# Turning the keys of a gated attention token-major: from TensorE transposes to VectorE block transposes with sixteen placing transfers

## The chip, the core and the metric

The kernel runs on one core of a Trainium2 chip. The metric is the device time of one launch in microseconds (us); smaller is better. The engines are named as a profile names them: PE (TensorE matmul) and PEld (its weight loads), DVE (VectorE), ACT (ScalarE), POOL (GpSimd), SP (SyncE, which here only issues DMA transfers). Each engine runs its own instruction list strictly in order and waits where an operand is not ready.

## The reference, cut to what matters

```python
def attn(q, k, v, a_re, a_im):                # all (4, 8, 768, 48)
    mag = np.sqrt(a_re * a_re + a_im * a_im)
    scale = np.minimum(mag, 0.999) / (mag + 1e-06)
    a_re_n, a_im_n = a_re * scale, a_im * scale
    for t in range(S):
        ar, ai = a_re_n[:, :, t, :, None], a_im_n[:, :, t, :, None]
        new_re = ar * S_re - ai * S_im
        new_im = ar * S_im + ai * S_re
        kv = np.einsum('bhd,bhe->bhde', k[:, :, t], v[:, :, t])
        S_re, S_im = new_re + kv, new_im
        y[:, :, t] = np.einsum('bhd,bhde->bhe', q[:, :, t], S_re)
    return y

x = attn_out.transpose(0, 2, 1, 3).reshape(3072, 384)
out = ((x @ w_a) * (x @ w_b)) @ w_out         # w_a, w_b: 384 x 1536, w_out: 1536 x 384
```

A recurrence over 768 tokens with a complex gate per key channel (8 heads of 48 channels, 4 sequences), then a gated feed-forward layer.

## The kernel before

**Units.** The recurrence is cut into chunks of 128 tokens. A *unit* u is one chunk of two sequences (256 tokens); there are 12 units, 6 per pair of sequences (`c = u % 6` is the chunk). Three stages follow one another for each unit:

- `prep(u)`, mostly DVE: it normalises the gates of unit u+1 (`scale`, whose first step is a square on ACT, L178, and whose first DVE step is L179, its last L193), builds running products of the gates of unit u (L211 to L294) and their inverse (L297 to L320), and multiplies keys and queries in the tile `qk` with them (L324, then twice L309). At its end it loads the gates of unit u+2 into a tile `a_t` (L158). There are two `a_t` buffers, and `prep(u)` uses the one of its own unit as scratch.
- `stack(u)`: ten transfers on SP that copy `qk` into `stk`, head by head, real part above imaginary part (96 rows a head).
- `attn(u)`, for each of the two sequences i and each group of four heads: `scores` (PE L379, mask on DVE L382 into `am`), `transposes` (PE L390 turns the stacked keys token-major, ACT L394 copies them out of PSUM into `kt`), `outputs` (PE L422 from `am`, values, state and queries into `xp`; ACT L424 rounds it into `xh`, DVE L430 leaves the rest in `xl`), and `state` (PE L445 from `kt` and the values, DVE L452 adds to the state tiles `u_111`, `u_112`). In the last chunk of a sequence `transposes` and `state` are left out.

**Passes.** The feed-forward layer of unit w is pass w: 12 blocks f. A block is 18 matmuls (L489, weights of `w_a` and `w_b` in two parts each), a gate product (ACT L497, DVE L498, ACT L499, DVE L500 give `hh` and `hl`), and six matmuls (L507) that run two blocks behind. A pass needs all of `xh` and `xl` of its unit. During pass w the generators of `attn(w+1)`, of the end of `prep(w+2)` and of the start of `prep(w+3)` are drained a piece at a time between blocks. PSUM has three buffers for the L489 results (`ab`) and two (`pm`) that scores, transposes and states share.

**What sets the order.** The program is written in this interleaved order, but a scheduler with a cost model then fixes each engine's list before the launch; `tc.high_priority` raises the gate product and the attention's copies above the rest. In the finished program nothing moves any more: who is late makes everything behind it on its engine late.

**Layouts that the change touches.** Values come as 128 columns for each pair of heads, with zero columns in the middle (32 + 16 + 16 + 32 used); state tiles have the same columns.

Of the kernel before, what the change touches and what calls it, by code (L numbers as in the profile page):

```python
# [8 lines left out]
F32 = mybir.dt.float32  # L9
# [8 lines left out]
B, H, S, D = 4, 8, 768, 48  # L18
DM, DF = 384, 1536
# [4 lines left out]
NJ = 3  # L24
# [43 lines left out]
def tile_kernel(ctx: ExitStack, tc: tile.TileContext, a_d, qk_d, v_d, w_d, qn_d, kn_d, vn_d, an_d, out_d):  # L68
# [98 lines left out]
    def scale(u, a_t, tmp):  # L167

        sc = zpool.tile([128, W], F32, name="sc")
        for n, hs in enumerate(halves if u == 0 else (slice(0, W),)):
            n = n and NU
            t = tmp[:, 0:2, hs]
            m, x, s0 = t[:, 0], t[:, 1], sc[:, hs]
            act.activation(out=t, in_=a_t[:, :, hs], func=AF.Square, accum_out=sums[:, u + n:u + n + 1])  # L178
# [12 lines left out]
            vec.scalar_tensor_tensor(out=s0, in0=m, scalar=0.5, in1=s0, op0=ALU.add, op1=ALU.mult)
            yield 900
            vec.scalar_tensor_tensor(out=s0, in0=s0, scalar=0.999, in1=x, op0=ALU.mult, op1=ALU.min)  # L193
            yield 900
        sc_tiles[u] = sc

    def rescaled(c):
        return c % 2 == 1 and c + 1 < NCH

    def prep(u):  # L200
# [137 lines left out]
    def stack(u):  # L338
        n = RUN if rescaled(u % NCH) else 2 * TOK
        for h in range(H):  # L340
            r0 = h * D
            while r0 < (h + 1) * D:
                j, p = divmod(r0, 128)
                m = min((h + 1) * D - r0, 128 - p)
                d0 = 2 * (r0 - h * D)
                sync.dma_start(out=stk[d0:d0 + 2 * m, h, 0:n], in_=qk[p:p + m, j, :, 0:n])
# [12 lines left out]
    quads = [[] for _ in range(4)]
    for g in range(H // 2):  # L360
        for q, pieces in ((3 * g, [(2 * g, 0)]), (3 * g + 1, [(2 * g + 1, 96)]),
                          (3 * g + 2, [(2 * g, 32), (2 * g + 1, 64)])):
            quads[q % 4].append((q // 4, [(h, g * 128 + off) for h, off in pieces]))

    def attn(u, xh, xl):

        c = u % NCH
        last = c + 1 == NCH
        ams, kts, xps = {}, {}, {}

        def cols(i):
            return slice(i * C, (i + 1) * C), slice(TOK + i * C, TOK + (i + 1) * C)
# [13 lines left out]
        def transposes(i, hg):  # L386
            qs, ks = cols(i)
            tp = ps_m.tile([128, 512], F32, name="pm")
            for h4 in range(4):
                pe.transpose(out=tp[:, h4 * KS:(h4 + 1) * KS], in_=stk[0:KS, hg * 4 + h4, ks],  # L390
                             identity=ident[0:KS, 0:KS])
            kt = kvp.tile([128, 4, KS], F32, name="kt", bufs=2)
            with tc.high_priority(offset=ATTN_FIRST):
                act.copy(out=kt.rearrange("p h k -> p (h k)"), in_=tp[:, 0:4 * KS])  # L394
# [42 lines left out]
        def state(i, hg):  # L437
            ut, v_t = us[i], v_tiles[u, i]
            own = u >= OWN_FROM
            n = D if own else 2 * D  # L440
            kp = ps_m.tile([128, 512], F32, name="pm")
            for h4 in range(4):
                h = hg * 4 + h4
                o = (h // 2) * 128 + (h % 2) * (80 if own else 32)
                pe.matmul(out=kp[0:KS, h4 * n:(h4 + 1) * n], lhsT=kts[i, hg][:, h4, :],  # L445
                          rhs=v_t[:, o:o + n], start=True, stop=True)
            uv = view(ut[0:KS], hg * 256, [[128, 2], [80, 2], [1, 48]])
            kv = view(kp[0:KS], 0, [[2 * n, 2], [D if own else 3 * D, 2], [1, D]])
            sv = view(stk[0:KS], hg * 4 * RUN + 2 * TOK + i, [[2 * RUN, 2], [RUN, 2], [0, 48]])
            with tc.high_priority(offset=ATTN_FIRST):  # L450
                if c > 0:
                    vec.tensor_tensor(out=uv, in0=kv, in1=uv, op=ALU.add)  # L452
                else:
                    act.copy(out=uv, in_=kv)
                if rescaled(c):
                    vec.tensor_tensor(out=uv, in0=uv, in1=sv, op=ALU.mult)
# [8 lines left out]
                     (residual, 1, 0), (state, 0, 0), (state, 0, 1), (transposes, 1, 0), (transposes, 1, 1),  # L465
                     (state, 1, 0), (state, 1, 1)]
        for fn, i, g in order:
            if not (last and fn in (transposes, state)):
                fn(i, g)
                yield  # L470

    def pieces(u):
        return 8 if u % NCH + 1 == NCH else 16

    def new_x():
        return (moe.tile([128, NJ, TOK], F32, name="xh"), moe.tile([128, NJ, TOK], F32, name="xl"))
# [3 lines left out]
        m, b = divmod(blk, NJ)  # L480
        return w_t[f, m][:, part, b * 128:(b + 1) * 128]

    def gemm1(f, xh, xl, ps_ab=ps_ab, moe=moe):
        ab = ps_ab.tile([128, 512], F32, name="ab")
        for m in range(2):
            n = 0
            for i in range(NJ):
                for part, xt in ((0, xh), (0, xl), (1, xh)):
                    pe.matmul(out=ab[:, m * TOK:(m + 1) * TOK],  # L489
                              lhsT=r(w_ab(f, part, m * NJ + i)),  # L490
                              rhs=r(xt[:, i, :]), start=n == 0, stop=n == 8)
                    n += 1
        h_t = moe.tile([128, TOK], F32, name="h_t")
        hh = moe.tile([128, TOK], F32, name="hh", bufs=HB)
        hl = moe.tile([128, TOK], F32, name="hl", bufs=HB)
        with tc.high_priority(offset=MOE_FIRST):
            act.copy(out=h_t, in_=ab[:, 0:TOK])  # L497
            vec.tensor_tensor(out=h_t, in0=ab[:, TOK:2 * TOK], in1=h_t, op=ALU.mult)  # L498
            act.copy(out=r(hh), in_=h_t)  # L499
            vec.tensor_tensor(out=r(hl), in0=h_t, in1=hh, op=ALU.subtract)  # L500
        return hh, hl
# [148 lines left out]
    for w in range(NU):  # L650
        last = w + 1 == NU
        x_nxt = None if last else new_x()
        at = None if last else attn(w + 1, *x_nxt)
        if not last:
            load_v(w + 1)
        os_ = [ps_o.tile([128, 512], F32, name=f"o{t}") for t in range(2)]
        slots = [0, 2 * (STACK_AT[min(w, 4)] + 1 - max(ATTN_AT[min(w, 4)], 0 if w else P1_AT + 1))]
        left = [pieces(w + 1)]

        def slot():  # L660
            if at is None or f < ATTN_AT[min(w, 4)] or (w == 0 and f <= P1_AT) or not slots[1]:
                return
            n = -(-left[0] // slots[1])
            slots[1] -= 1
            for _ in range(n):
                next(at, None)
                left[0] -= 1

        for f in range(NF):
            if w == 0:  # L670
                next(ws, None)
                drain(p1, P1_F)
                if f == P1_AT:
# [4 lines left out]
            pend.append((w, f, *gemm1(f, *x_cur), os_))  # L678
# [89 lines left out]
```

## Time and profile before

| | |
|---|---|
| median of 3 runs | 690.6 us (690.31 to 691.74) |
| the profiled execution | 690.18 us, of which 688.5 us are the span that the profile covers |
| granted TensorE clock | 0.972 of full speed over the span |
| instructions | 14290 |
| DMA packets | 30232, 63.94 MB |

The profile is of one execution. Its page gives busy time by engine, the span in 40 slices, the chain of work that ended last and the costliest groups of instructions. Further views are the windows (busy time by engine in a stretch of the span), the timeline of an engine, the waits and the list of DMA issues. A busy PE is not PE at its peak, since matmuls are pipelined: two matmuls of 280 ns each may start 120 ns apart.

### The profile page before, as it was taken

To read this page: it belongs to the slowest core of one execution; us is meant where nothing else is said; L and a number is where in the kernel's file an instruction comes from. 1 tells how busy PE (TensorE), PEld (TensorE's weight loads), DVE (VectorE), ACT (ScalarE), POOL (GpSimd) and SP (SyncE) were. 2 spreads that over 40 slices of the span, in tenths; PEclk is the share of its full clock that TensorE was granted. 3 is DMA by queue.
4 is the path that set the end of the run, shared out by engine and by line. 5 is a ranking of instruction groups with operands and counts; after the bars stand their busy time and mean duration, and the time that the engine had idled before them with its cause. 6 is when DMAs were issued, how large, how long until landed. Compare 5 with 4: busy or idle time off the path is not lost.

```text
span 688.5 us, 14290 instructions
## 1 busy us (share of the span) xinstructions
PE 644.5 (94%) x5842; PEld 608.3 (88%) x5842; DVE 550.1 (80%) x1259; ACT 310.1 (45%) x622; POOL 5.6 (1%) x11
## 2 busy tenths in 40 slices
PE   3547999999999999999999999999999999999996
PEld 1214889899999999999999999999999999999996
DVE  6999899998989989999898898999989963233221
ACT  7357664735445346354363553635542332221221
POOL 3000000000000000000000000000000000000000
PEclk9676999999999999999999999999999999999999
DMA  8963301513314225043160440611500500400000
GB/s 321 402 268 95 121 1 44 143 54 87 115 39 139 63 78 145 16 136 104 29 194 2 122 117 3 178 60 62 155 24 18 153 24 18 108 24 2 24 1 28
DMA packets 30232, 63.94 MB, mean 93 GB/s; under 512 B 3664, under 2 KB 7248, under 8 KB 30160
## 3 DMA queue, kind: packets, MB, share of 16 engines
q1 hardware_dynamic: 26704, 58.23, 27.3%
q10 hardware_dynamic: 3456, 4.72, 1.9%
q8 instruction: 48, 0.79, 0.5%
q14 instruction: 24, 0.20, 0.1%
HBM read 39.32 MB, written 4.72 MB: 64 GB/s over the span
## 4 chain that ended last, share of the span: by engine, by line
PE 66%; DVE 25%; ACT 4%; DMA 2%; issue 2%; SPq 0%; DVEq 0%; ACTq 0%
PE ab L489 33%; PE o L507 16%; PE xp L422 5%; PE pm L379 4%; PE pm L445 3%; DVE a_t L289 3%; DVE qk L309 2%; PE pm L390 2%; DVE h_t L498 2%; DVE hl L500 2%; PE pm L147 1%; DVE z L294 1%; DVE pr L227 1%; DVE am L382 1%; DVE pb L262 1%
## 5 line engine op out<-in xcount | busy, mean ns | idle before, releaser
L489 PE MATMUL ab<-xh,w 128*128 128x256 f32 x1728 | 341.6, 286 | 0.0
L489 PEld LDWEIGHTS ab<-xh,w 128*128 128x128 f32 x1728 | 277.2, 189 | 1.7 <-issue 0.8
L489 PE MATMUL ab<-xl,w 128*128 128x256 f32 x864 | 245.5, 284 | 0.0
L489 PEld LDWEIGHTS ab<-xl,w 128*128 128x128 f32 x864 | 163.0, 189 | 0.6 <-issue 0.2
L507 PE MATMUL o<-w,hh 128*128 128x384 f32 x576 | 152.7, 343 | 0.0
L497 ACT COPY h_t<-ab 128x256 f32<-128x256 f32 x144 | 53.4, 371 | 163.4 <-PE ab L489 163.4
L498 DVE TENSOR_TENSOR h_t<-ab,h_t 128x256 f32<-128x256 f32 x144 | 60.4, 420 | 64.6 <-ACT h_t L497 64.3
L507 PEld LDWEIGHTS o<-w,hh 128*128 128x128 f32 x576 | 96.6, 188 | 1.1 <-issue 1.0
L507 PE MATMUL o<-w,hl 128*128 128x384 f32 x288 | 97.2, 338 | 0.0
L499 ACT CAST hh<-h_t 128x256 fp32r<-128x256 f32 x144 | 58.0, 403 | 78.0 <-DVE h_t L498 76.9
L500 DVE TENSOR_TENSOR hl<-h_t,hh 128x256 fp32r<-128x256 f32 x144 | 60.4, 419 | 16.6 <-ACT hh L499 16.4
L379 PE MATMUL pm<-stk 128*128 128x128 f32 x384 | 54.8, 280 | 2.1 <-DMA stk<-qk 2.0
L147 PE MATMUL ab<-o_sb,ident 128*128 128x384 f32 x42 | 28.1, 764 | 29.7 <-DVE o_sb L138 29.7
L379 PEld LDWEIGHTS pm<-stk 128*128 128x128 f32 x384 | 50.2, 194 | 5.7 <-issue 3.6
L507 PEld LDWEIGHTS o<-w,hl 128*128 128x128 f32 x288 | 54.1, 188 | 0.0
L227 DVE TENSOR_TENSOR pr<-z 128x384 f32<-128x384 f32 (+1 forms) x91 | 47.2, 525 | 1.8
L289 DVE TENSOR_TENSOR a_t<-z,b_t 128x768 f32<-128x768 f32 x48 | 44.7, 947 | 0.1
L147 PEld LDWEIGHTS ab<-o_sb,ident 128*128 128x128 f32 x42 | 9.5, 268 | 39.3 <-DVE o_sb L138 30.3
L309 DVE TENSOR_TENSOR qk<-qk,z 128x1536 f32<-128x1536 f32 (+1 forms) x26 | 42.3, 1626 | 0.2
L422 PE MATMUL xp<-am,v_t 128*32 128x128 f32 x768 | 37.7, 281 | 4.3 <-DVE am L382 4.1
L382 DVE TENSOR_TENSOR am<-pm,mask 128x512 f32<-128x512 f32 x48 | 32.7, 685 | 5.2 <-PE pm L379 4.4
L424 ACT CAST xh<-xp 128x384 fp32r<-128x384 f32 x24 | 11.4, 475 | 49.3 <-PE xp L422 49.1
(107 smaller groups left out, 768.7 us busy)
## 6 DMA issues: line engine op xcount, KB each, us to landing
w<-in_dram SPq DMA_DIRECT2D x36, 384.0 KB, 8.0
qk<-in_dram SPq DMA_DIRECT2D x12, 768.0 KB, 4.9
stk<-qk SPq DMA_DIRECT2D x48, 192.0 KB, 3.3
a_t<-in_dram SPq DMA_DIRECT2D x11, 768.0 KB, 4.3
v_t<-in_dram SPq DMA_DIRECT2D x24, 256.0 KB, 2.7
stk<-qk SPq DMA_DIRECT2D x24, 192.8 KB, 3.3
out_dram<-o_sb ACTq DMA_DIRECT2D x24, 192.0 KB, 1.9
stk<-qk SPq DMA_DIRECT2D x16, 128.0 KB, 3.1
```

What stands on the lines that cost most here:

```text
L147: pe.matmul(out=lp[:, 0:n], lhsT=ident, rhs=t, start=True, stop=False)
L227: vec.tensor_tensor(out=pr[:, :, :, o:o + n], in0=view(zz, W + at_(i) + 2 * o, [[W, 2], [-W, 2], [2, n]]), in1=tok(slice(1, 3), i - 1, o, ...
L289: vec.tensor_tensor(out=pz[:, s].rearrange("p (j b e) -> p j b e", j=SUB // 2, e=2), in0=zb[:, 1 + s], in1=view(bb, (1 + k - s) * NB, [[0, ...
L309: vec.tensor_tensor(out=qk4[:, :, k, x0:x1], in0=qk4[:, :, 1, x0:x1], in1=z[:, k].rearrange("p (j t) -> p j t", j=NJ).unsqueeze(2).broadca ...
L379: pe.matmul(out=sp[:, h4], lhsT=stk[:, h, ks], rhs=stk[:, h, qs], start=True, stop=True)
L422: run = pe.matmul(out=xp[qd * 32:(qd + 1) * 32, ti], lhsT=l, rhs=rr, start=st, stop=sp_, tile_position=(0, qd * 32), skip_group_check=True ...
L489: pe.matmul(out=ab[:, m * TOK:(m + 1) * TOK], lhsT=r(w_ab(f, part, m * NJ + i)), rhs=r(xt[:, i, :]), start=n == 0, stop=n == 8)
L497: act.copy(out=h_t, in_=ab[:, 0:TOK])
L498: vec.tensor_tensor(out=h_t, in0=ab[:, TOK:2 * TOK], in1=h_t, op=ALU.mult)
L499: act.copy(out=r(hh), in_=h_t)
L500: vec.tensor_tensor(out=r(hl), in0=h_t, in1=hh, op=ALU.subtract)
L507: pe.matmul(out=os_[tt][:, 0:DM], lhsT=r(ht[:, ts]), rhs=r(w_t[f, 2][:, part, :]), start=(f == 0 and n == 0), stop=(f == NF - 1 and n == 2))
```

## The change

For units 2, 3, 4 and 6 to 10 (every unit from 2 on that has a `state` stage) the keys are no longer turned by PE and copied by ACT. Instead `prep(u)` ends with four DVE instructions (`turn_keys`, L385), each of which transposes the 32 x 32 blocks of the keys and writes them into the unit's `a_t` buffer, real and imaginary channels alternating; and `stack(u)` ends with sixteen more SP transfers (`place_keys`, L395) that move each block row to its place in `kt`, now one tile for the whole unit with one buffer. Since `a_t` of unit u is now read by these transfers, the load of unit u+2's gates into the same buffer comes behind them.

Values keep 112 columns for each pair of heads, so `load_v` issues two transfers a tile (64 and 48 columns) in place of one, and state tiles are 448 columns wide. The feed-forward's `h_t` has one buffer in place of two; from pass 1 on every other block takes its `h_t` from the ring of output tiles `o_sb`.

```diff
+VG = 112
+VW = H // 2 * VG
+KT_FROM = 2
...
-    us = [const.tile([128, 512], F32, name=f"u{i}") for i in range(2)]
+    us = [const.tile([128, VW], F32, name=f"u{i}") for i in range(2)]
...
         for k in range(2):
             times_p(k, 0 if u else 1, 2)
             yield 1670
+        if u >= KT_FROM and c + 1 < NCH:
+            yield from turn_keys(u, a_t)
+            turned[u] = a_t
         if 0 < u < NU - 2:
             a_tiles[u + 2] = load_a(u + 2)
...
     def stack(u):
...
+        if u in turned:
+            place_keys(u, turned.pop(u))
...
-            t = vpool.tile([128, 512], F32, name="v_t")
-            sync.dma_start(out=t, in_=v_d[u, i])
+            t = vpool.tile([128, VW], F32, name="v_t")
+            for c0, s0, n in ((0, 0, 64), (64, 80, 48)):
+                sync.dma_start(out=t.rearrange("p (g e) -> p g e", g=H // 2)[:, :, c0:c0 + n],
+                               in_=v_d[u, i].rearrange("p (g e) -> p g e", g=H // 2)[:, :, s0:s0 + n])
...
+    def new_kt(u):
+        kt_tiles[u] = kvp.tile([128, 2, H * KS], F32, name="kt", bufs=1)
+
+    def turn_keys(u, t):
+        for s in range(2):
+            for i in range(2):
+                vec.transpose(out=view(t[:], i * NJ * 64 + s, [[G * 64, 4], [64, NJ], [2, 32]]),
+                              in_=view(qk[:], s * RUN + TOK + i * C, [[32, 4], [2 * RUN, NJ], [1, 32]]))
+            yield 900
+
+    def place_keys(u, t):
+        new_kt(u)
+        src = t.rearrange("p s w -> p (s w)").rearrange("p (t g x) -> p t g x", t=4, g=G)
+        dst = kt_tiles[u].rearrange("p i (j b x) -> p (i j) b x", j=NJ, b=4)
+        for tb in range(4):
+            for pb in range(4):
+                sync.dma_start(out=dst[tb * 32:(tb + 1) * 32, :, pb], in_=src[pb * 32:(pb + 1) * 32, tb])
...
-            if not (last and fn in (transposes, state)):
+            if not (last and fn is state or fn is transposes and (last or u >= KT_FROM)):
...
-        h_t = moe.tile([128, TOK], F32, name="h_t")
+        if spare and f % 2:
+            h_t = moe.tile([128, DM], F32, name="o_sb", bufs=O_BUFS)[:, 0:TOK]
+        else:
+            h_t = moe.tile([128, TOK], F32, name="h_t", bufs=1)
```

Lines of the changed kernel lie 3 to 35 higher: L379 is now L413, L422 is L454, L445 is L477, L489 is L521, L507 is L542, L498 and L500 are L533 and L535, L179 is L182, L309 is L314, L158 is L161, L346 is L354, L336 is L344.

The scheduler's lists differ in more than the added and removed instructions. Three places:

**SP, between the stack transfers of two units.** Before, the load of `a_t` comes ahead of the ten `stk` transfers (here those of one unit, and the start of the next unit's):

```order
L158 DMA a_t<-in_dram 128x1536
L346 DMA stk<-qk 96x1x512 x2
L346 DMA stk<-qk 64x1x512
L346 DMA stk<-qk 32x1x512
L346 DMA stk<-qk 96x1x512 x2
L346 DMA stk<-qk 32x1x512
L346 DMA stk<-qk 64x1x512
L346 DMA stk<-qk 96x1x512 x2
L336 DMA qk<-in_dram 128x3x512
```

Now the same stretch of SP's list reads:

```order
L354 DMA stk<-qk 96x1x512 x2
L354 DMA stk<-qk 64x1x512
L354 DMA stk<-qk 32x1x512
L354 DMA stk<-qk 96x1x512 x2
L354 DMA stk<-qk 32x1x512
L354 DMA stk<-qk 64x1x512
L354 DMA stk<-qk 96x1x512 x2
L395 DMA kt<-a_t 32x6x64 x16
L344 DMA qk<-in_dram 128x3x512
L161 DMA a_t<-in_dram 128x1536
```

The sixteen placing transfers stand behind the stack, and the loads of `qk` and of `a_t` stand behind them; the load of `a_t` also waits until they have landed.

**DVE, early in `prep(8)`.** Before, the first step of the next unit's gate normalisation (L179) comes amid the second of the seven running products (L227, L233), close behind L211 with which the stage begins:

```order
L211 TENSOR_TENSOR z<-a_t,sc 128x96x4x2
L500 TENSOR_TENSOR hl<-h_t,hh 128x256
L227 TENSOR_TENSOR pr<-z 128x384
L233 TENSOR_TENSOR z<-pr 128x2x96
L227 TENSOR_TENSOR pr<-z 128x384
L179 SCALAR_TENSOR_TENSOR a_t<-a_t 128x768
```

Now that step (L182) stands behind every running product of the unit and behind the state updates of `attn(7)` (L484, L488), and the next step (L189) three feed-forward blocks later:

```order
L488 TENSOR_TENSOR u_112<-u_112,stk 96x2x2x48 x2
L182 SCALAR_TENSOR_TENSOR a_t<-a_t 128x768
L533 TENSOR_TENSOR h_t<-ab,h_t 128x256
L535 TENSOR_TENSOR hl<-h_t,hh 128x256
L533 TENSOR_TENSOR o_sb<-ab,o_sb 128x256
L535 TENSOR_TENSOR hl<-o_sb,hh 128x256
L533 TENSOR_TENSOR h_t<-ab,h_t 128x256
L535 TENSOR_TENSOR hl<-h_t,hh 128x256
L189 TENSOR_TENSOR a_t<-a_t 128x768
```

Further down the list, the two L314 that finish `prep(8)` stand behind the gate product of that pass's tenth block. The steps of `prep` that do not need the normalisation have moved ahead of it.

**PE, the attention of unit 7.** Before, it lies in pass 6 between blocks 7 and 9 of 12 (L489 and L507 are the feed-forward):

```order
L489 MATMUL ab<-xh,w_757 128x256
L379 MATMUL pm<-stk 128x128 x8
L507 MATMUL o_4818<-w_476,hh 128x384 x2
L507 MATMUL o_4818<-w_476,hl 128x384
L507 MATMUL o_4819<-w_476,hh 128x384 x2
L507 MATMUL o_4819<-w_476,hl 128x384
L489 MATMUL ab<-xh,w_815 128x256
L390 MATMUL pm<-ident,stk 128x96 x4
L489 MATMUL ab<-xl,w_815 128x256
```

Now all of it stands behind the twelfth block and behind the last L542 of pass 6, and directly ahead of pass 7. Eleven of its sixteen score matmuls and the first sequence's outputs come first, then these rows:

```order
L454 MATMUL xp<-stk,u_111 32x128 x4
L477 MATMUL pm<-v_t,kt 96x48
L413 MATMUL pm<-stk 128x128 x3
L477 MATMUL pm<-v_t,kt 96x48
L413 MATMUL pm<-stk 128x128
L477 MATMUL pm<-v_t,kt 96x48 x2
L454 MATMUL xp<-am,v_t 32x128 x4
L454 MATMUL xp<-stk,u_112 32x128 x4
```

A state matmul, which reads the placed keys `kt`, stands ahead of the last scores and of the second sequence's outputs, and no feed-forward matmul stands between. The attention of units 3, 4, 8, 9 and 10 stands in the same way at the ends of passes 2, 3, 7, 8 and 9; that of unit 5, which has no state, at the end of pass 4; that of unit 6 in pass 5 from block 8 on, its states and second outputs behind block 12; and of unit 2's the states and the second outputs have moved behind block 12 of pass 1.

More of the change, by code (lines that the diff above doesn't have):

```diff
@@ L195, in scale @@
         sc_tiles[u] = sc
+    turned = {}
     def rescaled(c):
@@ L360, in tile_kernel @@
     for g in range(H // 2):
-        for q, pieces in ((3 * g, [(2 * g, 0)]), (3 * g + 1, [(2 * g + 1, 96)]),
-                          (3 * g + 2, [(2 * g, 32), (2 * g + 1, 64)])):
-            quads[q % 4].append((q // 4, [(h, g * 128 + off) for h, off in pieces]))
+        for q, pieces in ((3 * g, [(2 * g, 0)]), (3 * g + 1, [(2 * g + 1, 80)]),
+                          (3 * g + 2, [(2 * g, 32), (2 * g + 1, 48)])):
+            quads[q % 4].append((q // 4, [(h, g * VG + off) for h, off in pieces]))
+    kt_tiles = {}
+    def new_kt(u):
[13 more added lines that the diff above has]
+                sync.dma_start(out=dst[tb * 32:(tb + 1) * 32, :, pb], in_=src[pb * 32:(pb + 1) * 32, tb])
     def attn(u, xh, xl):
@@ L368, in attn @@
         last = c + 1 == NCH
-        ams, kts, xps = {}, {}, {}
+        ams, xps = {}, {}
+        if not last and u < KT_FROM:
+            new_kt(u)
         def cols(i):
@@ L391, in transposes @@
                              identity=ident[0:KS, 0:KS])
-            kt = kvp.tile([128, 4, KS], F32, name="kt", bufs=2)
             with tc.high_priority(offset=ATTN_FIRST):
-                act.copy(out=kt.rearrange("p h k -> p (h k)"), in_=tp[:, 0:4 * KS])
-            kts[i, hg] = kt
+                act.copy(out=kt_tiles[u][:, i, hg * 4 * KS:(hg + 1) * 4 * KS], in_=tp[:, 0:4 * KS])
         def outputs(i, _):
@@ L443, in state @@
                 h = hg * 4 + h4
-                o = (h // 2) * 128 + (h % 2) * (80 if own else 32)
-                pe.matmul(out=kp[0:KS, h4 * n:(h4 + 1) * n], lhsT=kts[i, hg][:, h4, :],
+                o = (h // 2) * VG + (h % 2) * (64 if own else 16)
+                pe.matmul(out=kp[0:KS, h4 * n:(h4 + 1) * n], lhsT=kt_tiles[u][:, i, h * KS:(h + 1) * KS],
                           rhs=v_t[:, o:o + n], start=True, stop=True)
-            uv = view(ut[0:KS], hg * 256, [[128, 2], [80, 2], [1, 48]])
+            uv = view(ut[0:KS], hg * 2 * VG, [[VG, 2], [64, 2], [1, 48]])
             kv = view(kp[0:KS], 0, [[2 * n, 2], [D if own else 3 * D, 2], [1, D]])
@@ L472, in pieces @@
     def pieces(u):
-        return 8 if u % NCH + 1 == NCH else 16
+        return 8 if u % NCH + 1 == NCH else 12 if u >= KT_FROM else 16
     def new_x():
@@ L481, in w_ab, with gemm1 @@
         return w_t[f, m][:, part, b * 128:(b + 1) * 128]
-    def gemm1(f, xh, xl, ps_ab=ps_ab, moe=moe):
+    def gemm1(f, xh, xl, ps_ab=ps_ab, moe=moe, spare=False):
         ab = ps_ab.tile([128, 512], F32, name="ab")
@@ L677, in tile_kernel @@
                     pgen = prep(2)
-            pend.append((w, f, *gemm1(f, *x_cur), os_))
+            pend.append((w, f, *gemm1(f, *x_cur, spare=w > 0), os_))
             slot()
```

## The prediction

> **What bounds the kernel now.** I read the engines' totals first, then windows, then the chain in order of time. From the page:
>
> ```profile
> PE 644.5 (94%) x5842; PEld 608.3 (88%) x5842; DVE 550.1 (80%) x1259; ACT 310.1 (45%) x622; POOL 5.6 (1%) x11
> ```
>
> A share of the whole span mixes stages, so the windows matter more: from 122 us to the end of the last `prep`, and from there on. Columns are PE, PEld, DVE, ACT, POOL busy time, granted clock, DMA share, GB/s.
>
> ```profile
> 122.00:570.00 448.00, 443.68 (x4319) 433.24 (x4320) 405.30 (x905) 209.50 (x407) 0.00 (x0) 1.00 0.30 87
> 570.00:688.00 118.00, 112.75 (x1054) 110.74 (x1044) 32.03 (x73) 28.74 (x72) 0.00 (x0) 1.00 0.10 30
> ```
>
> In the first PE idles 4.3 us of 448; DVE is busy for 90% and idles 42.7 us. So PE bounds, with DVE close behind. The chain in order of time (start, length, what) shows how they hand over:
>
> ```profile
> 165.95 1.67 DVE qk L309
> 167.64 3.34 DMA stk<-qk
> ...
> 211.94 1.66 DVE qk L309
> 213.63 3.37 DMA stk<-qk
> 225.93 1.88 PE xp L422 x64
> 227.81 1.09 PE pm L379 x8
> ...
> 249.60 2.15 PE ab L489 x18
> 251.76 1.05 PE o L507 x6
> ```
>
> The end of `prep` (second L309, unit 2 at 167.6, unit 3 at 213.6) releases the stack, and everything else is PE: a feed-forward block takes 2.15 + 1.05 = 3.2 us. Starts of passes 2, 5, 6 and 10 (first L489), from PE's timeline:
>
> ```profile
> 194.87 0.36 PE L489 MATMUL ab<-xh,w 128*128 128x256 f32 x1
> 343.70 0.28 PE L489 MATMUL ab<-xh,w 128*128 128x256 f32 x1
> 392.88 0.28 PE L489 MATMUL ab<-xh,w 128*128 128x256 f32 x1
> 595.51 0.28 PE L489 MATMUL ab<-xh,w 128*128 128x256 f32 x1
> ```
>
> From pass 2 to pass 10 that is 400.6 us, 50.1 a pass. How much slack a late load has, from the timelines of SP and ACT:
>
> ```profile
> 209.89 0.33 SPq L158 DMA_DIRECT2D a_t<-in_dram  x1
> 213.63 6.65 SPq L346 DMA_DIRECT2D stk<-qk  x10
> 223.13 0.60 SPq L336 DMA_DIRECT2D qk<-in_dram  x1
> ```
>
> ```profile
> 216.38 1.49 ACT L178 ACTIVATE a_t<-a_t 128x1536 f32<-128x1536 f32 x1 [0.36 <-DVE z L211]
> ```
>
> The gates are fetched 3.7 us before the stack and squared at 216.4, which is 2.2 us after a 4.3 us load (below) has landed. That load is on nobody's path now, but with little to spare.
>
> **The change, part by part.** Groups of instructions (line, engine, shape, count, busy us, mean ns, idle before), and the DMA issues (KB each, median us to landing):
>
> ```profile
> L390 PE MATMUL pm<-ident,stk 96*128 96x96 f32 x160 | 20.0, 251 | 0.5 <-DVE am L382 0.5
> L394 ACT COPY kt<-pm 128x384 f32<-128x384 f32 x40 | 18.0, 482 | 7.9 <-PE pm L390 7.9
> L430 DVE TENSOR_TENSOR xl<-xp,xh 128x384 fp32r<-128x384 f32 x20 | 11.0, 552 | 11.7 <-ACT xh L424 11.6
> L134 DVE TENSOR_SCALAR o_sb<-w 128x384 uint32<-128x384 uint32 x36 | 12.5, 351 | 1.2 <-ACT w L142 0.6 <-DMA w<-in_dram 0.4
> L382 DVE TENSOR_TENSOR am<-pm,mask 128x512 f32<-128x512 f32 x48 | 32.7, 685 | 5.2 <-PE pm L379 4.4 <-PE xp L422 0.7
> ```
>
> ```profile
> stk<-qk SPq DMA_DIRECT2D x48, 192.0 KB, 3.3
> a_t<-in_dram SPq DMA_DIRECT2D x11, 768.0 KB, 4.3
> out_dram<-o_sb ACTq DMA_DIRECT2D x24, 192.0 KB, 1.9
> stk<-qk SPq DMA_DIRECT2D x16, 64.0 KB, 2.8
> ```
>
> *Removed.* 128 of the 160 PE transposes. The 20.0 us busy are with overlap: in PE's timeline near 70 us (quoted below) four take 0.50, of which 0.25 is the length of the last, so one starts 0.08 behind another. 8 units x 16 x 0.08 are 10.2 us of PE, 1.3 a unit. 32 ACT copies, 15.4 us of an engine at 45%: nothing.
>
> *Added on DVE.* 4 x 8 transposes of 384 elements. No row shows one; the bounds are the one-source 128x384 at 0.35 and the product over 1536 elements at 1.67 (L309 above). I take 0.55, the two-source 128x384: 17.6 us in all, 2.2 a unit. They stand behind the L309 that releases the stack, so the stack itself doesn't wait for them.
>
> *Added on SP.* 128 placing transfers of 48 KB. Ten stack transfers were issued in 6.65 us, 0.665 each. At that pace sixteen more take 10.6, and the last lands 3.3 after its issue. With T the end of `prep`, the keys are in place at K = T + 6.65 + 15 x 0.665 + 3.3 = T + 19.9. The ends: paced like a plain load (0.33) and landing like an output (1.9) K is T + 13.5; paced at 0.75, with the DVE transposes at 1.67 each so that SP starts at T + 9, T + 23.6. I take the middle one, since the stack is the same queue and the same kind of copy. The extra value transfers (24 more issues at some 0.33, waiting beside PE) I cost at nothing: a tile is fetched a pass ahead.
>
> *Added waits.* PE's list has a state matmul ahead of the second sequence's outputs, so PE stands at K, and with it the whole next pass, which needs `xh` and `xl`. From K: four state and four score matmuls (0.8 and 1.1), the mask (0.7), outputs (1.9), rounding (0.5): 5.0. After an idle stretch PE also runs slow. The one such place late enough to compare is near 70 us, behind a wait of 2.22:
>
> ```profile
> 69.79 1.93 PE L422 MATMUL xp<-am,v_t 128*32 128x128 f32 x32 [2.22 <-DVE am L382]
> 71.65 1.87 PE L379 MATMUL pm<-stk 128*128 128x128 f32 x8
> ...
> 73.54 0.50 PE L390 MATMUL pm<-ident,stk 96*128 96x96 f32 x4
> 74.40 1.08 PE L422 MATMUL xp<-am,v_t 128*32 128x128 f32 x32 [0.36 <-DVE am L382]
> ```
>
> ```profile
> 68.00:72.00 4.00, 2.21 (x33) 1.73 (x34) 3.29 (x6) 0.72 (x2) 0.00 (x0) 0.72 0.57 201
> ```
>
> In that window the granted clock (behind the busy times) is 0.72. The same outputs took 1.93 and then 1.08, the scores 1.87 and (row at 227.81) 1.09: 1.6 us lost. So the pass starts at S = K + 6.6 (ends 5.0 and 8).
>
> The load of `a_t` waits for K and lands at K + 4.3, just before ACT comes to the square: in itself it costs little there. Its price is what it did to DVE's list: both L314 (now the end of `prep`) stand behind the pass's tenth block. Three blocks' first matmuls come at once (3 x 2.15), the other seven at 3.2: block 10 ends at S + 28.9, then copy, product, L314, rest, L314 (0.4 + 0.4 + 1.7 + 0.4 + 1.7) give T = S + 33.6 at the least. Along DVE: the normalisation ends with block 5, at about S + 16.3, and from L289 to the end of L309 the trace has 18.8 us:
>
> ```profile
> 239.89 1.82 DVE L289 TENSOR_TENSOR a_t<-z,b_t 128x768 f32<-128x768 f32 x2
> ...
> 256.99 1.75 DVE L309 TENSOR_TENSOR qk<-qk,z 128x1536 f32<-128x1536 f32 x1
> ```
>
> That is S + 35.1; I take 35 (ends 33.6 and 36.5).
>
> *Sum.* One loop is 19.9 + 6.6 + 35 = 61.5 us where a pass took 50. T(2) = 167.6 stays. S(2) = 167.6 + 26.5 = 194.1, where the pass started before as well. S(3) = 255.6, S(4) = 317.1, T(5) = 352.1. Unit 5 has no state: stack landed (9.5, from 213.63 to 223.13), twice scores, mask and outputs (6.3), rounding 0.5, so S(5) = 368.4. Pass 5 loses its transposes alone: 49.2 - 1.3, S(6) = 416.3, with K(6) long past. Then three loops: S(7) = 477.8 (T(7) = 451.3), S(8) = 539.3, S(9) = 600.8, T(10) = 635.8. At the end of pass 9 DVE's list has the last mask of `attn(10)` behind most of `prep(11)`: four transposes, L211 to L318 with the masks, some 31 us from T by the durations above; then mask, outputs and both roundings, so S(10) = T(10) + 37 = 672.8. From S(10) to the end it was 688.5 - 595.5 = 93.0: a span of 765.8, and with the 1.7 us around the span, 767.5. This is against the profiled execution, 690.18, which is 0.4 below the median of the runs; I say 767. The single `h_t` buffer in pass 0 I cost at nothing: a block's copy then waits for the rest (L500) of the block before, which DVE's list has ahead of its product anyway; at worst it is 12 x 0.4.
>
> [...]
>
> **Rivals.**
>
> *Quick placing.* Sixteen short transfers with K = T + 13.5, no slow clock, T = S + 33.6: a loop of 52.1. S(2) = 193.6, S(4) = 297.8, S(6) = 395.6, S(9) = 551.9, S(10) = 620.5, end 713.5, time 715. For it: small copies may be issued as fast as loads. Against it: copies of 64 KB are in no row faster than 2.8.
>
> *DVE becomes the bound, nothing worse.* The waits of DVE between 122 and 570 us (total, times, longest):
>
> ```profile
> DVE a_t L303 <- ACT a_t L297: 9.8, 9, 1.6
> DVE h_t L498 <- ACT h_t L497: 9.1, 14, 1.9
> DVE a_t L318 <- ACT a_t L305: 4.6, 9, 1.2
> DVE hl L500 <- ACT hh L499: 4.6, 7, 1.0
> ```
>
> These 28.1 us are turns between ACT and DVE that stay. If the gates' lateness were hidden, DVE would need 405.3 + 17.6 + 28.1 = 451 us where the window has 448: 693. Against it: L314 behind block 10 is fixed.
>
> *Faster.* PE sheds 10.2 us and all waits stay hidden: 680. It decides at `prep`'s end: K must come before PE has done twelve blocks and their tail, S + 41.5, so T by S + 21.6. For it: before, units were stacked early enough for attention to start at block 7 of 12, and PE idled 1%. Against it: T can't come before S + 33.6 in this list.
>
> *Transfers one at a time.* If each placing transfer waited for the one before (2.8 us), K = T + 51.5 and six loops add 190: 957. [...] Against it: the stack's transfers overlap.
>
> **How the numbers follow.** Stalls at six passes as summed: 0.77; its upper ends together (K = T + 23.6, S = K + 8, T = S + 36.5, a loop of 68.1) give 811, and half of the way to the quick case 740. Quick placing: 0.09. DVE alone: 0.04. Faster: 0.05. No change within 0.2%, which is what a measurement of this kernel can tell: 0.02. Above 808, one at a time or worse: 0.03. The range 714 to 808 leaves out these last four, 0.14, and the corner above 808. Faster 0.05, same 0.02, slower 0.93.
>
> **What would show it.** PE idle time of 10 to 15 us at the ends of passes 2, 3, 6, 7, 8 and 9, released by a transfer into `kt` ahead of L477; the granted clock under 1 behind it; 61 us between the starts of passes; ten `stk` and sixteen `kt` transfers in 17 us; STREAM_TRANSPOSE near 0.55 us; ACT's L181 right behind `xh`. I am wrong if PE's gaps are under 3 us, if they are released by DVE alone, or if SP issues the sixteen in 5 us.

## The result: 771.05 us, and the profile after

| | before | changed |
|---|---|---|
| median of 4 runs each, us | 690.61 (690.31 to 691.74) | 771.05 (768.40 to 774.12) |
| ratio, 95% interval | | 1.1163 (1.1116 to 1.1209) |
| span of the profiled execution, us | 688.5 | 770.5 |
| granted TensorE clock over the span | 0.972 | 0.926 |

The forecast was 767 (714 to 808). The engines' totals of the changed kernel:

```profile
PE 667.5 (87%) x5714; PEld 622.4 (81%) x5714; DVE 575.6 (75%) x1291; ACT 294.9 (38%) x590; POOL 5.5 (1%) x11
```

128 matmuls fewer, and PE is busy for 23 us *more* (644.5 before). That is the first sign of a slow clock. First the transfers. T is again the end of `prep` (the end of its second L314), K the moment at which the placed keys let PE go on, S the start of the next pass. SP's timeline around the end of `prep(7)` (T = 457.4; start, length, what):

```profile
457.41 6.76 SPq L354 DMA_DIRECT2D stk<-qk  x10
464.28 11.56 SPq L395 DMA_DIRECT2D kt<-a_t  x16
475.88 0.60 SPq L344 DMA_DIRECT2D qk<-in_dram  x1
477.31 0.33 SPq L161 DMA_DIRECT2D a_t<-in_dram  x1
```

The load of the gates stood 3.7 us *ahead* of T before; it now comes 19.9 us behind it. PE's timeline in the same stretch, with what ended the idle time in brackets:

```profile
469.07 0.51 PE L454 MATMUL xp<-am,v_t 128*32 128x128 f32 x8 [1.88 <-DVE am L416]
...
476.07 0.50 PE L477 MATMUL pm<-v_t,kt 128*96 128x48 f32 x2 [3.50 <-DMA kt<-a_t]
...
484.44 0.48 PE L521 MATMUL ab<-xh,w 128*128 128x256 f32 x2
```

K, where the first state matmul finds the keys, is 476.1 = T + 18.7, and the next pass starts at S = 484.4 = K + 8.3. The windows of T to K, K to S, S to the next T, and of the whole pass (PE, PEld, DVE, ACT, POOL busy, granted clock, DMA share, GB/s):

```profile
457.40:476.10 18.70, 11.43 (x107) 9.15 (x106) 16.58 (x44) 2.10 (x4) 0.00 (x0) 0.91 0.56 125
476.10:484.40 8.30, 8.07 (x96) 7.38 (x96) 3.26 (x14) 1.19 (x2) 0.00 (x0) 0.59 0.61 199
484.40:518.80 34.40, 34.40 (x267) 34.40 (x267) 26.23 (x44) 16.79 (x34) 0.00 (x0) 1.00 0.10 26
...
484.40:546.00 61.60, 54.36 (x484) 52.27 (x483) 46.62 (x104) 21.16 (x43) 0.00 (x0) 0.92 0.30 79
```

and the same pass (7) before:

```profile
443.90:494.50 50.60, 50.47 (x498) 49.34 (x497) 48.44 (x109) 24.75 (x49) 0.00 (x0) 1.00 0.29 85
```

The pass takes 61.6 us for 50.6: 7.1 us more of idle PE, and 3.9 us more of busy PE, although the pass has 16 transposes less. The busy part goes with the clock: 0.59 between K and S above, 0.60 between K and S at the end of this pass (537.5 to 546.0). Between S and the next T PE is busy for all of the 34.40 us. PE's waits between 122 and 660 us (total, times, longest; a wait of 10.2 us for the last mask at the end of pass 9 lies behind that stretch):

```profile
PE pm L477 <- DMA kt<-a_t: 23.6, 6, 4.6
PE xp L454 <- DVE am L416: 13.7, 14, 1.9
PE pm L413 <- DMA stk<-qk: 10.5, 19, 1.5
```

### The profile page after: what moved, and what is told of

The parts are those of the page before. It is cut to its first block, busy times and chain, and to the rows that moved or that the text cites. A ratio compares the mean times of both kernels' runs of the same rounds, so it can differ in the third digit from the quotient of the medians.

```text
span 770.5 us, 14189 instructions
## 1 busy us (share of the span) xinstructions
PE 667.5 (87%) x5714; PEld 622.4 (81%) x5714; DVE 575.6 (75%) x1291; ACT 294.9 (38%) x590; POOL 5.5 (1%) x11
## 4 chain that ended last, share of the span: by engine, by line
PE 60%; DVE 21%; SPq 7%; DMA 5%; ACT 3%; issue 2%; DVEq 0%; ACTq 0%
PE ab L521 33%; PE o L542 13%; PE xp L454 6%; SPq L395 3%; PE pm L477 3%; DMA w<-in_dram 3%; DVE qk L314 3%; PE pm L413 3%; SPq L354 3%; DVE am L416 2%; DVE pr L232 2%; DMA stk<-qk 2%; DVE pb L267 1%; DVE a_t L294 1%; DVE b_t L273 1%
## 5 line engine op out<-in xcount | busy, mean ns | idle before, releaser
L521 PE MATMUL ab<-xh,w 128*128 128x256 f32 x1728 | 336.8, 284 | 0.6 <-ACT xh L456 0.6
L521 PEld LDWEIGHTS ab<-xh,w 128*128 128x128 f32 x1728 | 275.7, 189 | 2.3 <-ACT xh L456 0.9
L521 PE MATMUL ab<-xl,w 128*128 128x256 f32 x864 | 244.4, 284 | 0.9 <-DVE xl L462 0.9
L521 PEld LDWEIGHTS ab<-xl,w 128*128 128x128 f32 x864 | 162.9, 188 | 1.9 <-DVE xl L462 1.1
L542 PE MATMUL o<-w,hh 128*128 128x384 f32 x576 | 151.7, 341 | 0.0
L542 PEld LDWEIGHTS o<-w,hh 128*128 128x128 f32 x576 | 98.3, 188 | 0.5 <-ACT hh L534 0.4
L542 PE MATMUL o<-w,hl 128*128 128x384 f32 x288 | 97.5, 340 | 0.1
L413 PE MATMUL pm<-stk 128*128 128x128 f32 x384 | 69.7, 309 | 13.1 <-DMA stk<-qk 10.5
L413 PEld LDWEIGHTS pm<-stk 128*128 128x128 f32 x384 | 58.1, 210 | 23.0 <-issue 10.0
L454 PE MATMUL xp<-am,v_t 128*32 128x128 f32 x768 | 47.2, 338 | 26.7 <-DVE am L416 26.6
L532 ACT COPY h_t<-ab 128x256 f32<-128x256 f32 x78 | 29.0, 372 | 99.8 <-PE ab L521 98.0
L456 ACT CAST xh<-xp 128x384 fp32r<-128x384 f32 x24 | 11.5, 477 | 138.2 <-PE xp L454 138.2
L477 PEld LDWEIGHTS pm<-v_t,kt 128*96 128x96 f32 x320 | 36.4, 184 | 28.7 <-issue 28.3
L477 PE MATMUL pm<-v_t,kt 128*96 128x48 f32 (+1 forms) x320 | 38.7, 265 | 23.7 <-DMA kt<-a_t 23.6
L533 DVE TENSOR_TENSOR h_t<-ab,h_t 128x256 f32<-128x256 f32 x78 | 33.1, 424 | 34.0 <-ACT h_t L532 33.4
L542 PEld LDWEIGHTS o<-w,hl 128*128 128x128 f32 x288 | 54.0, 188 | 0.6 <-DVE hl L535 0.6
L454 PEld LDWEIGHTS xp<-am,v_t 128*32 128x32 f32 x768 | 26.5, 134 | 31.5 <-DVE am L416 29.3
L532 ACT COPY o_sb<-ab 128x256 f32<-128x256 f32 x66 | 24.3, 369 | 71.3 <-PE ab L521 71.2
L533 DVE TENSOR_TENSOR o_sb<-ab,o_sb 128x256 f32<-128x256 f32 x66 | 27.8, 422 | 27.5 <-ACT o_sb L532 26.9
L534 ACT CAST hh<-h_t 128x256 fp32r<-128x256 f32 x78 | 31.6, 405 | 41.9 <-DVE h_t L533 41.8
```

What stands on the lines that cost most here:

```text
L413: pe.matmul(out=sp[:, h4], lhsT=stk[:, h, ks], rhs=stk[:, h, qs], start=True, stop=True)
L454: run = pe.matmul(out=xp[qd * 32:(qd + 1) * 32, ti], lhsT=l, rhs=rr, start=st, stop=sp_, tile_position=(0, qd * 32), skip_group_check=True ...
L477: pe.matmul(out=kp[0:KS, h4 * n:(h4 + 1) * n], lhsT=kt_tiles[u][:, i, h * KS:(h + 1) * KS], rhs=v_t[:, o:o + n], start=True, stop=True)
L521: pe.matmul(out=ab[:, m * TOK:(m + 1) * TOK], lhsT=r(w_ab(f, part, m * NJ + i)), rhs=r(xt[:, i, :]), start=n == 0, stop=n == 8)
L542: pe.matmul(out=os_[tt][:, 0:DM], lhsT=r(ht[:, ts]), rhs=r(w_t[f, 2][:, part, :]), start=(f == 0 and n == 0), stop=(f == NF - 1 and n == 2))
```

## Experiments

The prediction's theory was: sixteen placing transfers stand in front of the state matmuls on PE, so PE and the next pass wait for K. The rival that the first runs brought up: the gate buffer `a_t` is held until K, so the gates of unit u+2 come late, and what `prep(u+1)` still has to do in that buffer comes late with them. Each kernel below is the changed one with the edit shown; "e1" to "e10" are used as names. "Load - T" is the start of the gates' load in SP's timeline minus the end of the second L314, and "T to T" the time between two such ends, both for units 2, 3, 4 and 6 to 9 (mean and range). "Scores" says how many of pass 6's twelve blocks PE has done, by its timeline, when the first score matmul of unit 7 starts.

| kernel | median us | ratio to before (95%) | load - T, us | T to T, us | scores |
|---|---|---|---|---|---|
| before | 690.6 | 1 | -3.8 | 41 to 46 | 7 |
| e3 side edits | 690.29 | 0.9996 (0.9985 to 1.0007) | -3.8 | 41 to 46 | 7 |
| e6 turned in `qk`, states last | 683.89 | 0.9884 (0.9868 to 0.9901) | -3.9 | 46 to 48 | 7 |
| e8 extra transposes | 707.61 | 1.0223 (1.0197 to 1.0248) | +3 | 47 to 55 | 7 |
| e10 one transfer | 687.38 | 0.9950 (0.9933 to 0.9967) | +11.5 | 50 to 51 | 8.7 |
| e4 eight transfers | 759.16 | 1.0996 (1.0969 to 1.1022) | +14.5 | 59 to 61 | 12 |
| changed | 771.05 | 1.1163 (1.1116 to 1.1209) | +19.7 | 60 to 63 | 12 |
| e1 states last | 804.72 | 1.1649 (1.1627 to 1.1672) | +19.7 | 67 to 70 | 12 |
| e9 hold, no wait for keys | 809.05 | 1.1714 (1.1684 to 1.1743) | +25.9 | 68 to 69 | 12 |

The rows fall into two groups. In the changed kernel, e1, e4 and e9 the attention of unit 7 (and of units 3 to 5 and 8 to 10, but for the first scores of unit 3 in e4) stands behind the twelfth block; in the others, and in e2, e5 and e7, it starts amid the blocks of its pass.

**e1: take the keys out of PE's way.**

```diff
-        for fn, i, g in order:
+        for fn, i, g in sorted(order, key=lambda o: u >= KT_FROM and o[0] is state):
```

> The changed kernel with one edit: from unit 2 on, the state matmuls stand last in a unit's attention, so no output waits for the placed keys. Theory 1 (the prediction's: PE standing at the keys is the price, and the late gates cost only through the list): the pass starts about 17 us after the end of prep in place of 27 (stack landed 9.5, scores, masks and outputs 6.3, rounding 0.5, some slow clock); 6 loops lose 9 to 10 us each, so 771 falls to about 710 to 715. Theory 2 (the held buffer: the gates of unit u+2 cannot be loaded before the keys of unit u have left that buffer, and from their landing to the end of the next prep there are some 36 us whatever PE does): the end of prep moves back in relation to the pass, S + 34 becomes S + 40 or later (the list has L314 behind the twelfth block), a loop is still 18 + 6 + 36 = 60 us, and the time stays at 750 to 770.

804.72 us: slower than the changed kernel, and above what either theory gave. No PE wait for `kt` is left; PE now waits for the stack, that is for the end of `prep` (between 76 us and the end of the last pass):

```profile
PE pm L413 <- DMA stk<-qk: 59.3, 19, 9.4
```

T is 481.5 here. SP's and DVE's timelines behind it:

```profile
488.41 11.15 SPq L395 DMA_DIRECT2D kt<-a_t  x16
499.60 0.60 SPq L344 DMA_DIRECT2D qk<-in_dram  x1
501.16 0.33 SPq L161 DMA_DIRECT2D a_t<-in_dram  x1
```

```profile
515.75 0.61 DVE L488 TENSOR_TENSOR u<-u,stk 96x192 f32<-96x192 f32 x2
518.33 0.42 DVE L533 TENSOR_TENSOR h_t<-ab,h_t 128x256 f32<-128x256 f32 x1 [1.97 <-ACT h_t L532]
519.80 0.96 DVE L182 SCALAR_TENSOR_TENSOR a_t<-a_t 128x768 f32<-128x768 f32 x1 [1.05 <-ACT a_t L181]
```

The gates are loaded as late as before this edit (T + 19.6), and their first DVE step stands behind the states, which have moved four blocks into the pass. The next end of `prep` is 549.5, 48.4 us behind the load. So taking away the wait at K, which the trace named, doesn't bring the loss back. Since the states have moved in DVE's list too, this run alone doesn't show what set the loop in the changed kernel.

**e9: hold the buffer, with no matmul behind it.** Keys are turned by PE and copied by ACT as before, without DVE transposes; the sixteen transfers read the gate buffer and write the half of `qk` that held the queries, so they also hold the load of the next keys.

```diff
-KT_FROM = 2
+KT_FROM = 12
-        if u >= KT_FROM and c + 1 < NCH:
-            yield from turn_keys(u, a_t)
+        if u >= 2 and c + 1 < NCH:
             turned[u] = a_t
-        dst = kt_tiles[u].rearrange(...)
+        dst = view(qk[:], 0, [[RUN, G], [64, 4], [1, 64]])
```

> The side edits of e3 with the keys turned by PE, copied by ACT, as before; no DVE transposes. In addition, behind each stack from unit 2 on that has a state, sixteen transfers of the changed kernel's shape (32 x 6 x 64 elements) read the unit's gate buffer and write the half of the keys tile that held the queries, which nobody reads any more. So no matmul waits for them; they only hold the gate buffer (and the load of the next keys, as in e6) until they have landed. Theory A (the held gate buffer by itself makes the loss, through the place that the scheduler gives to the end of prep and the attention): T + 18, 6 for the load of the gates, then 36 to 44 to the end of prep, in seven loops: 760 to 810. Theory B (the loss needs the wait for the keys in PE's list): 690 to 700, since that wait is gone.

809.05 us, at the top of what the held buffer was to give. No matmul reads what these transfers write, and yet all of the loss is there, and more. PE waits for the stack, not for keys (122 to 740 us):

```profile
PE pm L411 <- DMA stk<-qk: 52.0, 18, 8.3
```

SP from one end of `prep` to the next:

```profile
484.39 6.65 SPq L353 DMA_DIRECT2D stk<-qk  x10
491.88 11.41 SPq L393 DMA_DIRECT2D qk<-a_t  x16
505.07 5.25 SPq L365 DMA_DIRECT2D v_t<-in_dram  x3
510.50 0.48 SPq L161 DMA_DIRECT2D a_t<-in_dram  x1
...
553.40 6.71 SPq L353 DMA_DIRECT2D stk<-qk  x10
```

26 us to the load, 42.9 us from there to the next stack. Not all of the 26 us is the hold: the last of the sixteen, issued at 502.7, landed 2.0 us later, some 20 us behind T, and SP's list then has three loads of values ahead of the gates, with 5.0 us of waits for state matmuls (L475). That the next keys are held as well isn't the cause: in e6 below their load starts 27 us behind T, and that kernel loses nothing.

**e2: free the buffer, keep the transfers.** The turned keys go into scratch tiles, taken from the masks' ring of two `am` buffers, and sixteen transfers of the same shape read `qk`, so the keys that arrive are not turned.

```diff
-            yield from turn_keys(u, a_t)
-            turned[u] = a_t
+            yield from turn_keys(u, None)
+            turned[u] = qk[:, :, :, 0:2 * TOK]
...
-                vec.transpose(out=view(t[:], i * NJ * 64 + s, [[G * 64, 4], [64, NJ], [2, 32]]),
+                vec.transpose(out=kvp.tile([128, 512], F32, name="am", bufs=2)[:, 0:384].rearrange('p (t j c) -> p t j c', t=4, j=NJ),
```

> The changed kernel, but the turned keys are written into a small scratch tile and the sixteen transfers read the keys tile instead of the gate buffer; same number, shape and run length of transfers, same four DVE transposes. The gate buffer is free at once and its load stands ahead of the stack again. The keys that arrive are not turned, so the states' contents are wrong. Theory 2 (the held gate buffer is the cause): the attention goes back amid the blocks, no wait longer than 2 us at the keys, 680 to 700. Theory 1 (sixteen transfers in front of the state matmuls are the cause wherever the gates are): K = T + 18 still falls behind the twelfth block where T comes later than S + 24, stalls of a few us in six passes, 700 to 730. Theory 3 (the transfers' traffic or DVE's transposes are the cause): no change, above 755.

707.54 us (ratio 1.0229, 1.0210 to 1.0248). Passes 2, 3 and 6 to 9 take 49.0 to 49.5 us against 50.3 to 51.3 before (passes 4 and 5 46.9 and 48.4 against 47.1 and 49.2). All that is lost is in one place, the end of pass 1 (78.5 us for 52.1), where the states of unit 2 stand ahead of its second outputs and a mask stands behind the whole end of `prep(3)` in DVE's list:

```profile
217.53 0.66 PE L454 MATMUL xp<-am,v_t 128*32 128x128 f32 x8 [12.89 <-DVE am L416]
```

The time lies in the range of Theory 1 (700 to 730), but not as Theory 1 has it: PE never waits for `kt`. Theory 2 fits all passes but this one. So neither the 128 transfers nor the 18 us of DVE transposes cost anything in the other seven units. How much of the one stall comes from sharing the masks' buffers wasn't tried; e5, which doesn't share them, still has most of it.

**e5 to e7: free the buffer in a kernel that computes the whole reference.** The queries' half of `qk` is dead once the stack has been read; the transposes move behind the stack and write there.

```diff
-            yield from turn_keys(u, a_t)
-            turned[u] = a_t
+            turned[u] = view(qk[:], 0, [[RUN, 2 * NJ], [1, 4 * 64]])
...
         if u in turned:
+            for _ in turn_keys(u, qk): pass
             place_keys(u, turned.pop(u))
...
-  out=view(t[:], i * NJ * 64 + s, [[G * 64, 4], [64, NJ], [2, 32]])
+  out=view(t[:], i * NJ * RUN + s, [[64, 4], [RUN, NJ], [2, 32]])
```

> The changed kernel, whole in what it computes, with the turned keys in the half of the keys-and-queries tile that held the queries: the four DVE transposes come behind the stack transfers, the sixteen placing transfers read that half, and the gate buffer is free at the end of prep as in the kernel before. Theory A (what costs is the order that follows from the held gate buffer; 49.2 us a pass in e2): seven or eight passes near 49.2 us, but the states of unit 2 still stand ahead of the second sequence's outputs at the end of pass 1, so one stall of up to 27 us as in e2: 685 to 710. Theory B (the sixteen transfers in front of the state matmuls hold PE wherever they stand): K comes 9 us later than in the changed kernel in relation to the end of prep, so six stalls as long as there or longer: 750 or more.

> As e5, and the state matmuls last in a unit's attention (the edit of e1). In the list the states then stand some four blocks into the next pass and no output waits for the keys. Theory A: no stall at the keys, every pass with 1.2 to 1.3 us less than the 50.5 of before, 690.6 - 8 x 1.3 = 680, within 676 to 686. Theory B': DVE's 18 us of transposes and the later states make DVE the bound: 690 to 700. What e1 did (a step of the gates behind the states) comes back: above 750.

> As e6, from unit 3 on instead of unit 2: unit 2's keys are turned by PE as before. One unit less: Theory A says 1.3 us above e6 (681 to 682). Rival: the weights' loads and conversion in pass 0 and 1 make unit 2 the dear one, then below e6 by more than 2 us.

e5: 696.28 us (1.0065, 1.0048 to 1.0081); passes of 46.6 to 49.8 from pass 2 on, and one stall of some 16 us at the end of pass 1 as in e2. e6, with e1's edit on top, takes that stall away: 683.89 us, 1.2% under the kernel before. e7, from unit 3 on: 685.41 us (0.9908, 0.9891 to 0.9924), 1.5 above e6 where 1.3 was expected; the two intervals overlap, so all it shows is that unit 2 isn't a dear one. e1's edit costs 34 us on the held buffer and gains 12 on the free one. e6's SP timeline from before T = 446.5 to the next T = 493.0:

```profile
442.83 0.33 SPq L161 DMA_DIRECT2D a_t<-in_dram  x1
446.57 7.50 SPq L354 DMA_DIRECT2D stk<-qk  x10
460.43 11.62 SPq L396 DMA_DIRECT2D kt<-qk  x16
...
489.30 0.34 SPq L161 DMA_DIRECT2D a_t<-in_dram  x1
```

The last of the keys, issued at 471.4, land 2.1 us later at T + 27.0, where the changed kernel has T + 19.9, and PE's waits between 122 and 600 us are these, none for `kt`:

```profile
PE xp L455 <- DVE am L417: 3.8, 5, 2.0
PE pm L414 <- DMA stk<-qk: 3.0, 4, 1.3
PE pm L414 <- DVE am L417: 1.0, 1, 1.0
```

**e3: the side edits alone** (only `KT_FROM = 12`, more than the highest unit).

> Only the side edits: 112-column values and states with four value loads per unit, one kt tile, one h_t buffer with every other block in the ring of output tiles; keys turned by PE as before (threshold 12). All theories of the keys say 690.6 within 1.5 us. Rival: the single h_t buffer or the extra loads cost; then 693 or more, with waits of ACT's gate copy for a buffer.

690.29 us: the 112 columns, the extra value loads and the single `h_t` cost nothing.

**e8: DVE's transposes as an extra.** As e3, with `turn_keys` into the gate buffer from unit 2 on and no placing.

> Keys turned by PE as before (the side edits of e3), and in addition the four DVE transposes of each unit from 2 on into the gate buffer, with nothing placed from it. Prices the DVE transposes alone: 32 x 0.57 = 18 us of an engine that is busy for 90% of the middle. Hidden: 690 to 692. Half on the path: 699. All on the path: 708.

707.61 us, as if all of the 18 us lay on the path. But e6 and e10 have the same 32 transposes for nothing, and so has e2 in seven units. What differs is that here the load of the gates comes behind them, amid the stack, while DVE's list keeps the first step of the gates so early that it has to wait (122 to 700 us):

```profile
DVE a_t L182 <- ACT a_t L181: 9.3, 4, 4.6
```

If all of it lies on the path, that is about half of the 17 us; passes 6 and 7 (54.5 and 58.1 us) have most of the loss, with PE at a granted clock of 0.97 and 0.94. What makes the other half wasn't settled.

**e4 and e10: hold the buffer for less time.** Eight transfers of 3072-byte rows, or one of 6144-byte rows, carry the same bytes, to the wrong places.

```diff
-            for pb in range(4):
-                sync.dma_start(out=dst[...], in_=src[...])
+            for i in range(2):
+                sync.dma_start(out=kt_tiles[u][tb * 32:(tb + 1) * 32, i], in_=t[tb * 32:(tb + 1) * 32, i])
```

> The changed kernel with eight placing transfers in place of sixteen: the same bytes, but each of 32 rows of 3072 bytes from the gate buffer to the same rows (the keys arrive in the wrong places, so the states' contents are wrong). The lists are nearly the same; L314 stands behind the ninth block instead of the tenth. Theories 1 and 2 (issue time of SP is the term of K): K comes 8 x 0.72 = 5.8 us earlier, and in six or seven loops the time falls by 35 to 50 us, to 720 to 737. Rival (the transfers' landing or DVE's transposes set K, not the number of issues): 765 or more.

> The changed kernel with one placing transfer per unit in place of sixteen: 128 rows of 6144 bytes from the gate buffer straight into the keys' tile (the keys arrive in the wrong places, so the states' contents are wrong). The gate buffer is held for some 11 us behind the end of prep (ten stack issues 6.7, one more 0.6, landing 3 to 4) in place of 19.5. In the list the attention of a unit is back amid the blocks 9 to 11 of the pass. Theory A (a cycle of end of prep, release of the buffer, load of the gates, 41 to 46 us to the next end of prep): 11 + 42 to 45 = 53 to 56 us a unit in seven cycles against 44.5 before; the passes need 49.2, so 4 to 7 us more in six or seven passes: 705 to 735. Rival (the number of transfers on SP is the cause, the hold is not): 681 to 690.

e4: 759.16 us, outside both. The keys and the load of the gates come 5 us earlier, but a pass is as long as in the changed kernel (60.2 to 62.2 us); 9.4 of the 12 us gained are at the end of pass 9. In place of the keys, DVE now holds PE. PE's and DVE's rows at T = 575.2 + 21:

```profile
596.64 1.52 PE L477 MATMUL pm<-v_t,kt 128*96 128x48 f32 x8 [4.06 <-DVE u L484]
```

```profile
596.16 0.16 DVE L283 TENSOR_TENSOR chk<-n 128x6 f32<-128x6 f32 x1
596.24 0.35 DVE L484 TENSOR_TENSOR u<-pm,u 96x192 f32<-96x192 f32 x1
```

The first state update stands in DVE's list behind all of the next `prep` up to L283, and DVE comes to it 21 us after T, although the keys are there. The changed kernel has the same work ahead of its last mask (L416 at 600.8 beside K at 598.0, at the end of pass 8): two releases, close together. At the ends of passes 2, 3 and 6 that mask had to wait for scores behind K (0.6 to 1.1 us), at the ends of 7, 8 and 9 DVE came to it from its own list without a gap.

e10: 687.38 us, below the 705 to 735 of the buffer's cycle and inside the range of the rival that the number of transfers is the cause. That rival doesn't hold for all that: e2, e5 and e6 issue sixteen and have no such loss. Here the buffer is held until T + 11.4 (SP at T = 465.6):

```profile
465.66 6.68 SPq L354 DMA_DIRECT2D stk<-qk  x10
472.44 0.54 SPq L395 DMA_DIRECT2D kt<-a_t  x1
...
477.08 0.33 SPq L161 DMA_DIRECT2D a_t<-in_dram  x1
```

The next T is 38.7 us behind that load, T to T is 50.1, and that is just the length of a pass. So, as far as these two runs go, a held buffer isn't dear by the microsecond: while load - T and the some 39 us behind the load fit into a pass, it costs nothing; 3 us more (e4) and T to T is 60. In e4's list, as in the changed kernel's, the attention stands behind the twelfth block, and the passes and `prep` take turns.

## Why the prediction came out right, step by step

- **The total**: 767 against 771.05; a loop of 61.5 us against 60.2 to 63.3 between the starts of passes 2, 3, 4 and of 6 to 9. That it is so close is in part luck: in each loop K came 1.2 to 2.3 us earlier than summed, and S followed it 1.6 to 2.2 us later.
- **K = T + 19.9**: measured 17.6 to 18.7 in six units. The sixteen issues took 10.4 to 11.6 us (assumed 10.6). The landing was over-sized: 3.3 from the stack, 2.0 in the list of DMA issues:

```profile
kt<-a_t SPq DMA_DIRECT2D x128, 48.0 KB, 2.0
```

And PE doesn't wait for the last transfer, as the sum has it. The first state matmul reads the first 96 columns of `kt`, which are whole with the fourteenth; the chain of unit 7 goes through that one's landing, ahead of K = 476.07:

```profile
473.93 2.00 DMA kt<-a_t
```

The last one landed at T + 18.7 to T + 19.9, so the sum is nearly right for the release of the gate buffer.

- **S = K + 6.6**: measured 8.2 to 8.8 in five of them (for unit 10 the prediction has another sum, below). The term that was too small is the slow clock: 1.6 us from the one place near 70 us, where the clock was 0.72 over 4 us. Here it was 0.59 to 0.61 for the whole of K to S.
- **The next T = S + 35**: 34.3 to 34.4 in six of seven, 36.3 behind S(6). ACT's L181 came right behind `xh`, as said, and L314 behind the tenth block. (The sum's lower end is S + 33.5 by its own terms, 28.9 and 4.6, not 33.6.)
- **S(10) = T(10) + 37**: 37.2. **Pass 5** was 47.9, measured 50.2; the clock was 1.00, and PE idled for 2.9 us. S(5) = T(5) + 16.3 was 19.7, with 4.4 us of idle PE and a clock of 0.91. These are the largest misses.
- **DVE's transposes at 0.55 us**: 0.569.

```profile
L385 DVE STREAM_TRANSPOSE a_t<-qk x32: 536/569/580, 167.9 to 643.8; 128x384 f32<-128x384 f32 x32
```

- **The sign "PE idles 10 to 15 us at the keys"** failed in size: 2.96 to 4.6 us at the keys (the shortest is just under the 3 us that were to show the prediction wrong), 6.5 to 7.6 us a pass in all (17.1 in pass 9); the rest of the loss is in PE's busy time, at the low clock.
- **Transfers one at a time**: not so. SP took 0.604 us for one (the median) and 10.4 to 11.6 us for sixteen, and half of them landed within 2.0 us of their issue.
- **The extra value transfers and `h_t` at nothing**: right (e3). **Removed transposes at 1.3 us a unit**: right; e2's passes are 1.0 to 2.3 us shorter than the same ones before.

The weak step was the reason. As a sum along the list as it stood, the prediction is sound: it adds T to K, K to S and S to the next T, and from S to that T PE has no idle time, so the gates' load costs little in itself there, as the prediction said. It also named the late load as what had put both L314 behind the tenth block. What it didn't ask is whether the rest of that order, the attention behind the twelfth block, has the same origin; it put the price there on PE standing at the keys. e9 has the whole loss without any such wait, e1 takes the wait away and loses more, and e4 has the keys 5 us earlier and passes of the same length. What the changed kernel, e1, e4 and e9 share, and none of the others has, is a load of the gates 14.5 us or more behind T (the mean) and the attention behind the twelfth block. The sum came out because it was read from one order, whatever had made that order.

Unit 5 of the changed kernel places no keys: the gates' load stands 4.2 us ahead of its T, and the next T follows after 43.3 us, as in the kernel before. It lacks the hold and the wait for keys alike, so it doesn't tell the two apart; the experiments do.

The rival "faster, 680" was given 0.05 on the ground that T could not come earlier in this list. e6, which has another list, shows what it needed: not an earlier T but a free gate buffer, with which, and with the states last, keys that land at T + 27.0 are hidden.

Two things stay open. The runs show that the hold is enough for the loss, and the traces show the loss where the attention has moved. Why the scheduler's cost model moves it there was not looked into, and no run holds the buffer with the old order or has the new order with a free buffer, so the two are not priced apart. And the price of the slow clock was not tried by itself.

## What to carry to other kernels

When a change lets a transfer read a buffer that another load refills, write down the cycle through that buffer (release, reload, the work behind it, next release) and compare it with the length of the loop. Here the hold was free below that length (e10), and just above it (e4) the static order had tipped over and lost far more than the difference. The wait that a trace names at the end of such a loop may be only where the lateness shows; a run without that wait (e1, e9) tells whether the loss goes with it. A region that is already dead, here the queries behind the stack, was a cheaper place for a transfer's source than a buffer with a reload pending.

## What the hardware showed that was not expected

The granted clock fell to 0.50 not only behind the wait of 3.50 us for the keys, but ahead of it too, behind the wait of 1.88 us for a mask. Windows around these two waits (PE busy, granted clock, DMA share, GB/s):

```profile
465.90:469.30 3.40, 1.46 (x14) 1.00 0.50 91
469.30:472.70 3.40, 3.27 (x64) 0.50 0.32 52
472.70:476.10 3.40, 0.03 (x1) 1.00 0.48 79
476.10:479.50 3.40, 3.24 (x16) 0.50 0.70 171
479.50:482.90 3.40, 3.33 (x64) 0.50 0.78 314
```

A window in which PE was busy for 1.46 us of 3.4, its longest gap 1.88 us, was followed by one at a clock of 0.50; the one with 0.03 us of PE's work, which the wait of 3.50 us fills, was followed by two. How short a wait can be with the clock still falling behind it was not shown.
